# Attention backward for one query: the second half of a wide output product placed behind the V scores

One core of a Trainium2 chip. The metric is the time of one execution in device microseconds (us), lower is better. PE is the tensor engine, ACT the scalar engine, DVE the vector engine, SP the engine that issues the transfers; PSUM is the memory in which PE leaves its sums.

## The reference, cut to what matters

```python
# B = 1, H = 32 heads, Sq = 1 query, Skv = 8192 keys, Dh = 128, all bfloat16
def _fwd_reference(q, k, v):
    scale = q.shape[-1] ** -0.5
    scores = jnp.einsum('bhqd,bhkd->bhqk', q, k) * scale
    attn = _softmax(scores, axis=-1)
    return jnp.einsum('bhqk,bhkd->bhqd', attn, v)

def reference(q, k, v, grad_out):
    _out, _vjp = jax.vjp(_f, q, k, v)     # _f calls _fwd_reference
    return (_out, *_vjp(grad_out))        # out, dq, dk, dv
```

Per head, K and V (2.097 MB each) are read, and dK and dV, just as large, are written. With one query, dK and dV are outer products, and every other product has a vector on one side.

## The kernel before

The heads are a software pipeline: in pass `h`, the K work of head `h` is mixed with the dQ and dK work of head `h-1`, and then the V work of head `h` follows. The order of instructions on each engine is the order of the program text. All tile transfers are issued by one engine (SP), in program order; SP waits at each until its buffer or its data is ready.

The output of a head is the product of the probabilities with V. Most heads do it in 64 narrow matmuls with V as weights (`contract`). Nine "wide" heads (2, 5, 8, ... 26) take V as the moving operand in 16 matmuls of 4x512. The sum then stands in PSUM tile `s`, ACT copies it to `four`, and 8 KB go to scratch memory:

```python
    def o_wide(h, first, last):
        x = st[h]
        for g in range(first, last):
            nc.tensor.matmul(x["s"][0:R, :], lhsT=x["p"][:, R * g:R * (g + 1), 0],
                             rhs=Vt[h][:, R * g:R * (g + 1), :].rearrange("p n d -> p (n d)"),
                             start=(g == 0), stop=(g == NT // R - 1), skip_group_check=True)
        if last == NT // R:
            four = small.tile([R, R * D], F32, tag="four", name="four")
            nc.scalar.copy(four[:], x["s"][0:R, :])
            nc.sync.dma_start(scratch[WIDE.index(h), 0:R * R * D].rearrange("(a c) -> a c", a=R), four[:])
```

`s` has one buffer, V two, K three, and the gradient tiles dK and dV two each. The part of pass `h` that matters:

```python
        # ... K scores, softmax, first V transposes of head h; dQ, dK of head h-1 ...
        v_copy(h, 0)
        v_transposes(h, 1)                 # each is 8 transposes on PE and a copy on ACT
        if h in WIDE:
            o_wide(h, 0, 8)
        v_transposes(h, 2)
        if h in WIDE:
            o_wide(h, 8, 16)               # <- what moves
        else:
            contract(Vt[h], x["p"], x["m"][:, 2:3])
            nc.scalar.copy(o_all[:, h:h + 1], x["m"][:, 2:3])
        v_scores(h, 0)
        v_scores(h, 1)
        v_transposes(h, 3)
        # ... (a small matmul in plain heads)
        v_scores(h, 2)
        v_scores(h, 3)                     # waits for ACT's copy of the transposes 3
        outer(h, "dv", 0); outer(h, "dv", 1); outer(h, "dv", 2)      # DVE
        if 0 < h and h + 2 < H:
            load_v(h + 2)                  # needs V's buffer of head h
        outer(h, "dv", 3)                  # and the store of dV
        # next pass: rows_bc(h+1) writes `s` on PE, XK transposes on DVE,
        # pd_of(h) (a reduction of the V scores on DVE, then a matmul), K scores of h+1
```

## Time and profile before

| | |
|---|---|
| time, median of the first 3 runs | 646.6 us (646.49 to 646.83) |
| bytes moved, mean rate | 269.85 MB, 419 GB/s |
| busy share: main DMA queue, DVE, PE, ACT | 98.2%, 79%, 77%, 29% |

To read the pages: a strip has 40 slices of the span, 16.1 us each. In a chain or timeline a row is start, length, engine, line of the kernel, and output<-inputs; what ended an idle time before the row stands in brackets. L218 is the wide product, L206 the V scores, L194 the V transposes, L256 the row broadcast of the next head, L163 its K scores, L223 ACT's copy of the sum. A "DMA" row in the chain is the time from a transfer's issue to its landing.

### The profile page before, as it was taken

The page shows a single profiled execution, that of the slowest core. Times are in us where ns is not written, and L with a number is a line of the kernel's source. Part 1 is how long each engine was busy: PE and PEld are TensorE (multiplying, and loading weights), DVE is VectorE, ACT ScalarE, POOL GpSimd, SP SyncE. Part 2 cuts the span into 40 slices and gives each one's busy share as a digit, 9 for nine tenths or more (in the row PEclk, how much of TensorE's full clock was granted, in tenths as well). Part 3 has the DMA queues.
Part 4 walks back from the last instruction along what each step waited for, and adds up shares of the span by engine and source line. Part 5 has one row for each costly group of instructions (what it writes and reads, how often), then busy time and mean ns, then how long its engine had stood idle before and what let it go on. Part 6 is the DMA issues. An engine that isn't in the chain of part 4 may idle for free.

```text
span 644.6 us, 20121 instructions
## 1 busy us (share of the span) xinstructions
PE 495.5 (77%) x9242; PEld 432.6 (67%) x9242; DVE 508.7 (79%) x673; ACT 184.3 (29%) x333; POOL 0.7 (0%) x6
## 2 busy tenths in 40 slices
PE   3998888886777977788777788877787787877780
PEld 2886876785676776658665776767586666866670
DVE  5998989877977778877789777797777987778870
ACT  2333333322233231233222332313322133321230
POOL 0000000000000000000000000000000000000000
PEclk9768668765766765686558666666865586665665
DMA  8999999999999999999999999999999999999995
GB/s 349 406 426 432 425 423 428 427 429 427 430 427 429 426 432 424 430 428 425 430 425 430 429 428 427 430 425 429 428 430 426 429 427 430 428 429 428 426 379 213
DMA packets 19833, 269.85 MB, mean 419 GB/s; under 512 B 2397, under 2 KB 2433, under 8 KB 2981
## 3 DMA queue, kind: packets, MB, share of 16 engines
q1 hardware_dynamic: 19701, 268.56, 98.2%
q8 instruction: 72, 1.18, 0.7%
q14 instruction: 12, 0.10, 0.0%
q10 hardware_dynamic: 48, 0.01, 0.0%
HBM read 134.25 MB, written 134.31 MB: 417 GB/s over the span
## 4 chain that ended last, share of the span: by engine, by line
DMA 61%; PE 27%; DVE 7%; ACT 1%; issue 1%; SPq 0%; DVEq 0%; ACTq 0%
DMA Vt<-in_v_dram 60%; PE T_ps L194 15%; DVE XK_sb L152 3%; DVE G_dv L241 3%; PE s_ps L218 3%; PE m_ps L211 2%; PE dp_ps L206 2%; PE s_ps L163 2%; PE dp_ps L211 1%; DMA Kt<-in_k_dram 1%; PE m_ps L328 1%; DVE G_dk L241 1%; ACT XT_sb L185 0%; ACT p_rep L337 0%; PE s_ps L179 0%
## 5 line engine op out<-in xcount | busy, mean ns | idle before, releaser
L194 PE MATMUL T_ps<-ident_f,Vt 128*128 128x128 f32 x1024 | 209.5, 373 | 26.1 <-DMA Vt<-in_v_dram 24.4
L194 PEld LDWEIGHTS T_ps<-ident_f,Vt 128*128 128x128 f32 x1024 | 176.1, 201 | 44.8 <-PE m_ps L316 26.7
L241 DVE TENSOR_TENSOR G_dv<-p_rep,qd 128x2048 bf16<-128x2048 bf16 x128 | 148.2, 1220 | 58.8 <-DMA out_dram<-G_dv 48.2
L241 DVE TENSOR_TENSOR G_dk<-ds_rep,qd 128x2048 bf16<-128x2048 bf16 x128 | 155.7, 1219 | 1.6 <-DMA out_dram<-G_dk 0.5
L185 ACT COPY XT_sb<-T_ps 128x1024 f32<-128x1024 f32 x128 | 128.3, 1007 | 91.6 <-PE T_ps L194 88.0
L152 DVE STREAM_TRANSPOSE XK_sb<-Kt 128x1024 f32<-128x1024 f32 x128 | 149.3, 1217 | 6.2 <-DMA Kt<-in_k_dram 5.7
L163 PE MATMUL s_ps<-q_blk,XK_sb 128*128 128x4 bf16 x2048 | 59.6, 168 | 75.3 <-DVE pdt L265 68.2
L163 PEld LDWEIGHTS <-XK_sb 128*128 128x128 bf16 x2048 | 56.9, 104 | 82.7 <-DVE pdt L265 75.4
L206 PE MATMUL dp_ps<-do_blk,XT_sb 128*128 128x2 bf16 x2048 | 66.5, 164 | 19.7 <-ACT XT_sb L185 19.7
L206 PEld LDWEIGHTS <-XT_sb 128*128 128x128 bf16 x2048 | 63.7, 101 | 26.4 <-ACT XT_sb L185 22.4
L211 PE MATMUL dp_ps<-ds_rep,Kt 128*128 128x1 bf16 x2048 | 64.0, 165 | 0.0
L211 PEld LDWEIGHTS <-Kt 128*128 128x128 bf16 x2048 | 59.5, 104 | 5.4 <-issue 5.3
L275 ACT COPY dq_all<-dp_ps 128x1 f32<-128x1 f32 x32 | 5.1, 159 | 193.2 <-PE dp_ps L211 186.3
L211 PEld LDWEIGHTS <-Vt 128*128 128x128 bf16 x1472 | 41.3, 97 | 0.6
L211 PE MATMUL m_ps<-p_rep,Vt 128*128 128x1 bf16 x1472 | 40.8, 164 | 0.0
L218 PE MATMUL s_ps<-Vt,p_rep 128*4 128x512 bf16 x144 | 36.4, 398 | 0.0
L337 ACT ACTIVATE p_rep<-e,rinv 128x256 bf16<-128x256 f32 x32 | 16.3, 509 | 63.3 <-DVE rinv L335 63.3
L335 DVE RECIPROCAL rinv<-m_ps 128x1 f32<-128x1 f32 x32 | 5.4, 168 | 33.8 <-PE m_ps L328 33.7
L218 PEld LDWEIGHTS <-p_rep 128*4 128x4 bf16 x144 | 11.2, 87 | 20.1 <-issue 6.0
L260 ACT CAST qd<-s_ps 128x256 bf16<-128x256 f32 x32 | 11.9, 372 | 31.0 <-PE s_ps L256 31.0
L327 ACT ACTIVATE e<-s_ps,nbias 128x64 f32<-128x64 f32 x32 | 10.0, 314 | 32.2 <-DVE nbias L323 32.2
L169 DVE TENSOR_TENSOR sm<-s_ps,in_quad 128x256 f32<-128x256 f32 x32 | 13.6, 425 | 6.5 <-PE s_ps L163 3.6
(56 smaller groups left out, 191.4 us busy)
## 6 DMA issues: line engine op xcount, KB each, us to landing
Vt<-in_v_dram SPq DMA_DIRECT2D x32, 2048.0 KB
Kt<-in_k_dram SPq DMA_DIRECT2D x31, 2048.0 KB
out_dram<-G_dv SPq DMA_DIRECT2D x30, 2048.0 KB
out_dram<-G_dk SPq DMA_DIRECT2D x30, 2048.0 KB
out_dram<-G_dv SPq DMA_DIRECT2D x4, 1024.0 KB
out_dram<-G_dk SPq DMA_DIRECT2D x4, 1024.0 KB
Kt<-in_k_dram SPq DMA_DIRECT2D x4, 512.0 KB
scratch<-four SPq DMA_DIRECT2D x9, 8.0 KB
```

What stands on the lines that cost most here:

```text
L152: nc.vector.transpose(XK[h][:, :, :, u, :], slots(Kt[h], u, NCH).rearrange("p g d -> p (g d)").bitcast(F32).rearrange("p (g w j) -> p g w ...
L163: nc.tensor.matmul(out[:, g, :], lhsT=cols[:, g, c // 2, c % 2], rhs=q_blk[:, h, c, :], start=(c == 0), stop=(c == 2 * NB - 1), skip_group ...
L169: nc.vector.tensor_tensor(x["sm"][:], x["s"][:, 0:NT].rearrange("p (a g) -> p a g", a=NQ).unsqueeze(2) .to_broadcast([P, NQ, NCH, CH]), in ...
L185: nc.scalar.copy(X[:], st[h].pop("T")[:])
L194: nc.tensor.transpose(T_ps[:, i, :], words[:, m * P:(m + 1) * P], ident_f[:])
L206: nc.tensor.matmul(st[h]["dp"][:, n:n + 2], lhsT=X[:, i, e2, :], rhs=do_blk[:, h, e2, :], start=(e2 == 0), stop=(e2 == 1), skip_group_chec ...
L211: nc.tensor.matmul(out_col, lhsT=Xt[:, n, :], rhs=rep[:, n, 0:1], start=(n == 0), stop=(n == NT - 1), skip_group_check=True)
L218: nc.tensor.matmul(x["s"][0:R, :], lhsT=x["p"][:, R * g:R * (g + 1), 0], rhs=Vt[h][:, R * g:R * (g + 1), :].rearrange("p n d -> p (n d)"), ...
L241: nc.vector.tensor_tensor(slots(G, r, 4).rearrange("p n (a b) -> p n a b", b=R), slots(rep, r, 4).unsqueeze(2).to_broadcast([P, Q, D // R, ...
L260: nc.scalar.copy(x["qd"][:].rearrange("p a d -> p (a d)"), x["s"][:, 256:512])
L327: nc.scalar.activation(e[:], x["sn"], ACT.Exp, bias=nbias[:], scale=scale, accum_out=rs[:])
L337: nc.scalar.activation(x["p"][:], e[:].unsqueeze(2).to_broadcast([P, NT, R]), ACT.Copy, scale=rinv[:])
```

## The change

Its evident intent is to let the V scores start sooner, so that the reduction behind them doesn't wait. No work is added or removed.

```diff
@@ -342,9 +342,7 @@
         if h in WIDE:
             o_wide(h, 0, 8)
         v_transposes(h, 2)
-        if h in WIDE:
-            o_wide(h, 8, 16)
-        else:
+        if h not in WIDE:
             contract(Vt[h], x["p"], x["m"][:, 2:3])
             nc.scalar.copy(o_all[:, h:h + 1], x["m"][:, 2:3])
         v_scores(h, 0)
@@ -355,6 +353,8 @@
         v_scores(h, 2)
         v_scores(h, 3)
+        if h in WIDE:
+            o_wide(h, 8, 16)
         outer(h, "dv", 0)
```

## The prediction

> **What bounds the kernel now.** I first read the page's strips and its queue table, because they tell whether anything is saturated. The first strip is the busy share of the 16 DMA engines in 40 slices of 16.1 us.
>
> ```profile
> DMA  8999999999999999999999999999999999999995
> GB/s 349 406 426 432 425 423 428 427 429 427 430 427 429 426 432 424 430 428 425 430 425 430 429 428 427 430 425 429 428 430 426 429 427 430 428 429 428 426 379 213
> ...
> q1 hardware_dynamic: 19701, 268.56, 98.2%
> ```
>
> The transfers are at 90% or more from the second slice to the last but one, at an even 423 to 432 GB/s, and the one queue that carries all tiles takes 98.2% of the engines' time. No compute engine is near that (DVE 79%, PE 77%, ACT 29%). Per head the kernel moves four tiles of 2.097 MB (K and V in, dK and dV out), 8.389 MB; at 428 GB/s, the mean of each 100 us stretch from 100 to 600 us, that is 19.6 us a head, and 32 heads are 627 us. The remaining 19 us of the span are the slower first and last slices.
>
> Then I read the chain that ended last, in order of time, around one wide head (head 14, of 2, 5, 8, ... 26) and the plain heads on both sides of it. Columns: start us, length us, what.
>
> ```profile
> 303.97 30.30 DMA Vt<-in_v_dram
> ...
> 341.08 1.82 PE s_ps L218 x8
> 342.89 0.89 PE dp_ps L206 x32
> 343.78 0.95 PE T_ps L194 x8
> 344.73 0.02 issue
> 344.75 29.17 DMA Vt<-in_v_dram
> 373.92 0.14 issue
> ...
> 383.21 30.53 DMA Vt<-in_v_dram
> 413.74 0.14 issue
> ```
>
> The page puts 60% of the span on "DMA Vt<-in_v_dram", and these lines show why that must not be read as a latency: a 2 MB load takes 4.9 us of all engines (2.097 MB / 428 GB/s) but 29 to 30.5 us from issue to landing. The other 24 to 25 us are four or five earlier 2 MB transfers ahead of it. The loads land at 334.27, 373.92 and 413.74, that is 39.65 and 39.82 us apart, which is two heads' worth of bytes (16.78 MB / 428 GB/s = 39.2 us) within 2%. The decisive comparison: from the start of a head's V transposes to the issue of the next V load takes 9.16 us in a plain head (374.05 to 383.21) and 10.34 us in the wide head (334.41 to 344.75). The wide head already issues 1.2 us later, its load waits about 1.2 us less (29.17 against 30.30 and 30.53), and the landing comes in step all the same. **The queue is elastic: a later issue shortens the time in it.**
>
> **What the Trainium skill says.** "DMA: Bandwidth & Descriptors", section "Where 436 GB/s comes from", gives 435.2 GB/s as the ceiling of the 16 ports; the steady 428 GB/s here is 98% of it, so I take the transfers as saturated. The same page, "Queues, rings and completion order", says that descriptors on one engine are consumed in ring order; the trace agrees as far as it can, the V load of 323.89 landing at 354.2 and the dV store issued right after it (324.32) releasing its buffer at 359.2, one tile's 5 us later. "Perfetto Trace Analysis", "DMA Instruction — HWDGE (DVE, Sync)", says that the data movement lies outside the profiled window of the issuing instruction; the issues last 0.33 us here against 29 us to landing, so I judge by landings.
>
> **The change part by part.** Nothing is added or removed. Nine times, eight 128x512 matmuls move from before the V scores to behind the last, and with them ACT's copy of the sum and the 8 KB store that follow. The built order of the sync and vector queues is the same as before; ACT changes by one place (the copy of the sum moves behind the fourth XT copy), PE by the move itself. The tensor line around the place, before (start, length, engine, line):
>
> ```profile
> 341.01 1.89 PE L218 MATMUL s_ps<-Vt,p_rep 128*4 128x512 bf16 x8
> 342.83 0.95 PE L206 MATMUL dp_ps<-do_blk,XT_sb 128*128 128x2 bf16 x32
> 343.64 1.07 PE L194 MATMUL T_ps<-ident_f,Vt 128*128 128x128 f32 x8
> 344.55 0.54 PE L206 MATMUL dp_ps<-do_blk,XT_sb 128*128 128x2 bf16 x16
> 345.87 0.55 PE L206 MATMUL dp_ps<-do_blk,XT_sb 128*128 128x2 bf16 x16 [0.78 <-ACT XT_sb L185]
> 346.36 0.28 PE L256 MATMUL s_ps<-rows,ident 32*128 32x256 bf16 x1
> 347.85 0.38 PE L232 MATMUL m_ps<-pd,ones_s 128*128 128x1 f32 x2 [1.22 <-DVE pd L230]
> 349.01 0.35 PE L163 MATMUL s_ps<-q_blk,XK_sb 128*128 128x4 bf16 x7 [0.78 <-DVE pdt L265]
> ```
>
> - The eight matmuls take 1.82 us start to start (341.01 to 342.83), 228 ns each. Without them in front, the V scores, the last transposes and ACT's fourth copy all come 1.82 us sooner. Its inputs allow that: the third XT copy ends at 342.12 and the third scores would want it at about 342.7. The fourth copy still takes 1.01 us, so the gap of 0.78 us in front of the last scores stays: the moved matmuls stand behind that gap and do not fill it. The last scores would end near 346.4 - 1.8 = 344.55, the eight matmuls near 346.45.
> - ACT's copy of the sum (576 ns, from the row of that tile) then runs from 346.5 to 347.05 in place of 342.93 to 343.51.
> - **A new wait on PE.** The next head's row broadcast (346.36) writes the buffer that this copy reads, of which there is one. It moves to about 347.1, so 0.75 us of PE idleness is new per wide head, 9 x 0.75 = 6.8 us in all. But the matmul behind it waits until 347.85 for DVE anyway, so the broadcast (0.28 to 0.39 us) still fits and the K scores at 349.01 stay. ACT's cast of the broadcast comes 0.75 us later and is first used by the next head's outer products, microseconds after.
> - **A later release of V.** The moved matmuls become the last readers of the V tile. On the sync queue the 8 KB store comes first, then the V load, then the dV store. These issued at 343.53, 344.75 and 345.17; I expect 347.1, 347.4 and 347.8. Two 2 MB transfers thus start waiting 2.65 us later, nine times. The next K load (353.07) is untouched.
> - What of it lies on the path that sets the end: before the V load of 344.75 about 24 us of transfers are queued, and 24 - 2.65 is still over 20. The thinnest queue at a wide head is at head 2. Up to its V load at 57.70, thirteen tiles (27.3 MB) have been issued. By the strip some 23.1 MB have been moved (16.1 us each at 349, 406 and 426 GB/s, and 9.4 us at 432), which leaves 4.2 MB or 9.8 us, still over three times the delay. So the engines never run dry, the order is the same, and the bytes are the same: 0 us. The last wide head is 26, five heads from the end; the tail (V landing at 612.7, then the last stores) has no moved work.
>
> Sum: 9 x 2.65 = 24 us of later issues, all taken from waiting in the queue, and 6.8 us of new PE idleness beside DMA. On the end: 0, with a few tenths either way.
>
> **The rivals.**
> 1. *The chain of waits is right and the V load's 29 us are a fixed latency.* Then each later release would carry through. Wide heads alternate between the two V buffers, so each buffer's loop would take 4 or 5 of the 9 delays, 4.5 x 2.65 = 12 us, 658.5 us (+1.8%). The 60% speaks for it; the comparison of wide and plain heads above speaks against it. I give it about 1%.
> 2. *PE or DVE becomes the bound through the new buffer wait.* If the row broadcast held up the K scores by the whole 0.75 us, a head would lengthen by that much: 6.8 us, 653.4 us. The 1.2 us that PE waits for DVE behind it speaks against it, and so does DVE, which sits idle 48.2 us in 22 waits for dV stores: compute has slack to make a delay up in the same head.
> 3. *A gain from earlier V scores.* They end 1.8 us sooner, so the vector engine's reduction of them never waits. That wait is 2.3 us in 2 places, all told, and in early heads the new broadcast wait would give back about as much; behind saturated transfers it is worth 0.
> 4. *The dV store's delay holds up the dV product two heads later,* which waits for its buffer (the 48.2 us above). The store keeps its place in the queue, so it should land at the same time: 0.
>
> **Range and chances.** The estimate is the time before, 646.6 us. The three runs lay within 0.34 us. I allow about 0.15% for a slightly different mix of reads and writes in the queue and for the early heads: 645.7 to 647.6 us. Faster by over 2% needs fewer bytes or a better rate, neither touched: 0.5%. Slower by over 2% needs more than rival 1 in full: 0.5%.
>
> **What would show it right or wrong.** In the profile after: DMA share and GB/s strip unchanged; in the chain the V loads issued by wide heads shortened from about 29.2 to about 26.5 us with the landings still 39.6 to 39.8 us apart; the row broadcast at PE with a new wait of some 0.75 us for ACT's copy, near 7 us in nine; the three sync issues 2.6 to 3.6 us later within the head; the K scores not later. The prediction is wrong if landings move apart to 42 us after wide heads, if the DMA strip shows a slice under 9 in the middle, or if the K scores of the next head move by the new wait and DMA's rate falls with them.

## More of the kernel before

The granted clock is the share of its full speed that PE was allowed.

## The result, and the profile after

After: 646.03 us median of 4 runs (645.96 to 646.93); before in the same rounds 646.72 us (646.49 to 647.59). The ratio is 0.999, 95% interval 0.9973 to 1.0007: the same. A ratio is the mean time of one kernel's runs over that of the other's of the same rounds, so not quite the ratio of the medians.

The page after, strips of DMA share and GB/s, and the queue's row:

```profile
DMA  8999999999999999999999999999999999999985
GB/s 338 419 423 430 426 427 426 425 424 421 427 408 428 428 428 431 423 431 429 426 426 432 426 428 429 428 427 430 424 430 428 430 424 431 425 431 427 430 376 235
...
q1 hardware_dynamic: 19701, 268.56, 98.3%
```

The transfers are as busy as before. One slice, of 177 to 193 us, has 408 GB/s; no issue is late there, and I don't know its cause. The profiled run happens to be the slowest of the four (646.93 us).

The chain after, around the same wide head as in the prediction (start, length, what):

```profile
305.64 29.49 DMA Vt<-in_v_dram
...
345.25 0.55 PE dp_ps L206 x16
345.80 1.83 PE s_ps L218 x8
347.64 0.02 issue
347.66 0.58 ACT four L223
348.24 0.04 issue
348.29 0.26 PE s_ps L256
348.55 0.06 PE m_ps L232
348.61 26.85 DMA Vt<-in_v_dram
375.47 0.14 issue
...
384.76 29.59 DMA Vt<-in_v_dram
```

The head's last link before the V load is now scores, wide product, copy of the sum, row broadcast. The load is issued 13.35 us after the start of the head's V transposes (335.26) instead of 10.34 us, and it waits 26.85 us instead of 29.17: 3.0 us later in, 2.3 us shorter. Over the nine wide heads the two traces give 3.2 us later and 3.4 us shorter on average. (This head is head 17. The prediction calls it 14, a miscount of mine; nothing in the working depends on it.)

The tensor engine's timeline after, around the moved matmuls:

```profile
343.02 1.07 PE L194 MATMUL T_ps<-ident_f,Vt 128*128 128x128 f32 x8
343.93 0.54 PE L206 MATMUL dp_ps<-do_blk,XT_sb 128*128 128x2 bf16 x16
345.25 0.55 PE L206 MATMUL dp_ps<-do_blk,XT_sb 128*128 128x2 bf16 x16 [0.78 <-ACT XT_sb L185]
345.74 1.89 PE L218 MATMUL s_ps<-Vt,p_rep 128*4 128x512 bf16 x8
348.29 0.26 PE L256 MATMUL s_ps<-rows,ident 32*128 32x256 bf16 x1 [0.66 <-ACT four L223]
348.55 0.38 PE L232 MATMUL m_ps<-pd,ones_s 128*128 128x1 f32 x2
349.71 1.84 PE L163 MATMUL s_ps<-q_blk,XK_sb 128*128 128x4 bf16 x64 [0.78 <-DVE pdt L265]
```

The gap of 0.78 us in front of the last V scores is still there, and a new gap of 0.66 us stands in front of the row broadcast, which waits for ACT's copy of `s`. The broadcast is 1.1 us later within the head than before, but the matmul behind it had waited 1.22 us for DVE. The K scores come 14.45 us after the head's V start (335.26 to 349.71), before 14.60 us.

### The profile page after: what moved, and what is told of

It reads as the page before. It is cut to its first block, busy times and chain, and to the rows that moved or that the text cites. A ratio compares the mean times of both kernels' runs of the same rounds, so it can differ in the third digit from the quotient of the medians.

```text
span 644.9 us, 20121 instructions
## 1 busy us (share of the span) xinstructions
PE 501.1 (78%) x9242; PEld 435.4 (68%) x9242; DVE 509.1 (79%) x673; ACT 184.6 (29%) x333; POOL 0.7 (0%) x6
## 4 chain that ended last, share of the span: by engine, by line
DMA 59%; PE 29%; DVE 5%; ACT 2%; issue 1%; SPq 0%; DVEq 0%; ACTq 0%
DMA Vt<-in_v_dram 58%; PE T_ps L194 16%; PE s_ps L218 3%; PE m_ps L211 3%; PE dp_ps L206 3%; DVE XK_sb L152 2%; DVE G_dv L241 2%; PE s_ps L163 2%; PE dp_ps L211 1%; ACT XT_sb L185 1%; DMA Kt<-in_k_dram 1%; PE m_ps L328 1%; DVE G_dk L241 1%; ACT four L223 0%; ACT p_rep L337 0%
## 5 line engine op out<-in xcount | busy, mean ns | idle before, releaser
L194 PE MATMUL T_ps<-ident_f,Vt 128*128 128x128 f32 x1024 | 211.7, 376 | 26.4 <-DMA Vt<-in_v_dram 24.3
L194 PEld LDWEIGHTS T_ps<-ident_f,Vt 128*128 128x128 f32 x1024 | 177.6, 202 | 45.2 <-PE m_ps L316 18.7
L206 PEld LDWEIGHTS <-XT_sb 128*128 128x128 bf16 x2048 | 65.1, 102 | 22.1 <-ACT XT_sb L185 21.9
L218 PE MATMUL s_ps<-Vt,p_rep 128*4 128x512 bf16 x144 | 41.4, 440 | 0.0
L267 DVE SCALAR_TENSOR_TENSOR ds_rep<-dp_ps,pdt,p_s 128x256 bf16<-128x256 f32 x32 | 15.5, 484 | 3.5 <-PE dp_ps L206 0.5
```

The source lines that it names most:

```text
L194: nc.tensor.transpose(T_ps[:, i, :], words[:, m * P:(m + 1) * P], ident_f[:])
L206: nc.tensor.matmul(st[h]["dp"][:, n:n + 2], lhsT=X[:, i, e2, :], rhs=do_blk[:, h, e2, :], start=(e2 == 0), stop=(e2 == 1), skip_group_chec ...
L267: nc.vector.scalar_tensor_tensor(out=x["ds"][:], in0=x["dp"][:, 0:NT].unsqueeze(2).to_broadcast([P, NT, R]), scalar=pdt[:], in1=x["p_s"][: ...
```

## The experiments

The theory: the 16 DMA engines' bytes set the time. The moved matmuls make V and dV go out later, the queue in front of the transfers is shortened by that, and what the order does to compute is hidden. The expectations call this the queue theory. Its rivals: the wait behind a V load is a latency; or the order does change compute, but in two directions that cancel; or V's buffers are the bound.

### Both orders where the transfers don't bind

`light_before` and `light_after` store only the first quarter of each dK and dV tile. Most of those outputs is never written, so their results are wrong (out and dq remain right). All the compute is there.

```diff
-            nc.sync.dma_start(rows_of(dst, h, c, parts), slots(G, c, parts))
+            if r == 3:
+                nc.sync.dma_start(rows_of(dst, h, 0, 4), slots(G, 0, 4))
```

> The order of before with only a quarter of every dK and dV tile stored (wrong result on purpose), so 5.2 MB a head in place of 8.4 and about 12.3 us of transfers. Queue theory: the transfers stop binding and the heads run at the compute pace of the early heads before (16.4 us plain, 17.8 us wide), so about 555 us (545 to 570), and a V load lands within 5 to 12 us of its issue instead of 29. Fixed-latency rival: the V loads still take about 29 us from issue to landing and the time stays near 640 us.

> The same with the order of after. This shows what the move is worth where compute binds. By the early heads of the two traces, from the third V transposes of a wide head to the next K scores it is 7.93 us before and 7.72 after at equal clock: 9 x 0.2 = 1.9 us quicker than light_before (0.3%). Rival (the new wait for ACT's copy costs more than the earlier V scores give): 0.3 to 0.6 us slower per wide head, 3 to 5 us (0.5 to 1%). If the moved matmuls run at the lower clock more often than before, that adds up to 1.6 us per head to the slower side.

Measured: light_before 569.15 us (5 runs, 567.67 to 573.51), ratio to before 0.8816 (0.8790 to 0.8842); light_after 570.32 us (568.04 to 572.60), ratio 0.8818 (0.8796 to 0.8839). The page of light_before, its strip of GB/s and its chain by engine:

```profile
GB/s 339 402 415 329 317 312 246 250 343 325 286 288 304 331 342 290 286 300 266 339 324 284 291 307 326 346 266 302 295 288 348 315 275 269 306 329 315 289 72 78
...
PE 51%; DVE 40%; ACT 4%; issue 3%; DMA 1%; SPq 0%; DVEq 0%; ACTq 0%
```

With 100 MB less to move, 12% of the time goes, though no instruction of compute was taken away; DMA leaves the chain (61% to 1%). So the bytes bind in the full kernel. The landing of single V loads, of which the expectation speaks, is in no view of `prof` here, since nothing waits for them any more. But the packed trace keeps sixteen completion stamps for each 2 MB transfer, and the last of them is the landing that the chain shows (373.92 us for the V load of 344.75 in before). By these stamps the V loads issued in light_before after the first 20 us land 8.7 to 10.8 us after their issue (only the first takes 14.8), where before takes 28.4 to 31.2 us from head 6 on. The wait shrinks with the bytes, so it is no fixed latency. I had the time 14 us too low: the wide heads take 18.6 us on average, not 17.8, and some plain ones 18 to 19.

The two orders are equal here as well, and the trace shows two effects of opposite sign. From the first wide matmul of a head to the DVE copy that starts the next head's chain (`pdt`) it is 9.61 us in light_before whenever both groups run at full clock; the shortest in light_after is 9.56 us, with its first group a little slow (2.02 us), and in the full kernel after 9.43 us (head 5) against 9.61 before. That is the 0.2 us expected. But in light_after the moved group ran slow in three of nine heads. Its timeline in one of them:

```profile
418.19 0.55 PE L206 MATMUL dp_ps<-do_blk,XT_sb 128*128 128x2 bf16 x16 [0.78 <-ACT XT_sb L185]
418.67 3.34 PE L218 MATMUL s_ps<-Vt,p_rep 128*4 128x512 bf16 x8
422.68 0.26 PE L257 MATMUL s_ps<-rows,ident 32*128 32x256 bf16 x1 [0.66 <-ACT four L223]
```

Eight matmuls take 3.34 us here and 1.89 us elsewhere. In the full kernel after, such a group (3.45 us, from 227.02 us) lay in a stretch with a mean granted clock of 0.53, while another (345.74 us) had 1.00. In light_before the second group took 1.89 us in all nine heads. The mean over the nine heads, slow groups on either side included, is 9.93 us in light_before and 10.31 us in light_after. Nine times 0.38 us is 3.4 us, yet the profiled spans are 567.0 and 566.7 us: the rest of the heads took as much less, which this study doesn't explain. Whether the place behind the gap lowers the clock, or the phase of the throttle happened to fall so, one profile each doesn't settle.

### Between the third and the fourth scores

`light_between` and `full_between` put the second eight matmuls into the gap of 0.78 us.

```diff
         v_scores(h, 2)
-        v_scores(h, 3)
         if h in WIDE:
             o_wide(h, 8, 16)
+        v_scores(h, 3)
```

> The same with the second eight matmuls between the third and the fourth V scores, in the gap of 0.78 us that the fourth scores wait for ACT's copy. Expected 0.5 us per wide head quicker than light_after, 4 to 5 us (0.8%), as the gap is filled and the copy of the sum no longer stands in front of the row broadcast. Rival: DVE's own chain binds there and it is equal to light_before within 1 us.

> That order with all stores. Queue theory: the same as before and after, 646.5 us within 0.8, whatever light_between shows, since the transfers still bind. Rival (compute order carries to the end): as much quicker as light_between is, 4 to 5 us.

Measured: light_between 556.95 us (4 runs, 556.19 to 559.22), ratio 0.8620 (0.8604 to 0.8636), so 12 us under light_before. full_between 645.84 us (645.82 to 645.96), correct, ratio to before 0.9989 (0.9976 to 1.0003): the same. The tensor engine in a wide head of light_between:

```profile
206.76 0.54 PE L206 MATMUL dp_ps<-do_blk,XT_sb 128*128 128x2 bf16 x16
207.23 1.89 PE L218 MATMUL s_ps<-Vt,p_rep 128*4 128x512 bf16 x8
209.05 0.55 PE L206 MATMUL dp_ps<-do_blk,XT_sb 128*128 128x2 bf16 x16
209.78 0.26 PE L257 MATMUL s_ps<-rows,ident 32*128 32x256 bf16 x1 [0.18 <-ACT four L223]
```

Both gaps are gone or nearly so: the scores wait no more for ACT (their copy runs beside the wide product), and the broadcast waits 0.18 us for the copy of the sum. From the first wide matmul to `pdt` it is 8.66 us at full clock, 0.95 under light_before, 9.04 us on average. That is 9 x 0.9 = 8 us of the 12. From K scores to K scores, 10 us of the 12 are in the wide heads (18.55 and 17.43 us on average) and 2 us in the plain ones, for which I have no cause. I had expected 4 to 5 us. **This is the sharpest pair: an order that is worth 12 us where compute binds is worth nothing that can be told from the spread (0.8 us, interval over 1) where the bytes bind.**

### A third V buffer

```diff
-V_BUFS = 2
+V_BUFS = 3
```

> Before with three V buffers in place of two, so V is released far ahead and its load can be issued a head earlier. Queue theory: the load only waits longer, time 646.6 within 1.5 us. Fixed-latency rival (V's release to landing is the loop that binds): a large gain, 20 to 30% of the span.

Measured: 646.56 us (646.40 to 646.68), before in the same rounds 646.56 us, ratio 0.9999 (0.9984 to 1.0014). V's buffers are not the bound, although 60% of the chain goes through V loads. The load did only wait longer: the last V load was issued 7.6 us earlier than in before (574.90 and 582.51 us) and landed at the same time (612.93 and 612.73 us).

### All V loads later

`late_v` is the order of before, with the V loads moved behind the next pass's K load.

```diff
@@ behind the K load of pass h
+        if 1 < h and h + 1 < 26:
+            load_v(h + 1)
@@ where the V load was
-        if 0 < h and h + 2 < H:
+        if 0 < h and h + 2 < H and h + 2 >= 26:
             load_v(h + 2)
```

> The order of before, but every V load up to head 25 is issued behind the next head's K load, some 8 to 9 us later, in plain and wide heads alike. Queue theory: the wait from issue to landing shrinks by as much as the issue is late (to about 20 us), landings stay about 39.7 us apart, time 646.6 us within 2. Fixed-latency rival: each of the two V loops takes 11 or 12 delays of 8.5 us: about 740 us.

Measured: 651.32 us (651.22 to 651.70), ratio 1.0075 (1.0058 to 1.0092). V loads on its chain:

```profile
162.03 23.26 DMA Vt<-in_v_dram
202.09 23.61 DMA Vt<-in_v_dram
243.61 21.72 DMA Vt<-in_v_dram
```

They wait about 7 us less, and the time is 89 us below what a fixed latency would make of it: that rival falls. But it isn't free, as I had expected within 2 us: 4.8 us were lost. What is known of this loss follows below.

### How much later is too late

`fill50` and `fill130` take the order of after and put 50 or 130 more 128x256 matmuls on V in front of the moved eight, in wide heads only, into columns of `m` that nobody reads. The results are correct.

```diff
+            for g in range(50):     # or 130
+                nc.tensor.matmul(x["m"][0:R, 256:512], lhsT=x["p"][:, R * (g % 16):R * (g % 16 + 1), 0],
+                                 rhs=Vt[h][:, 2 * (g % 32):2 * (g % 32 + 1), :].rearrange("p n d -> p (n d)"),
+                                 start=True, stop=True, skip_group_check=True)
             o_wide(h, 8, 16)
```

> The order of after with 50 further 128x256 matmuls from V in front of the moved eight, in the nine wide heads only (their sums are never read; the result stays right). At 114 ns each (half of the 228 ns of a 128x512) that is 5.7 us more PE time on the path to the V release and to the next head. Three heads take 3 x 19.8 = 59.4 us by the transfers and 2 x 16.4 + 17.8 = 50.6 us by compute, so 8.8 us of slack per wide head: the same within 1%. Rival (the release is on the path): 9 x 5.7 / 2 = 26 us slower, or 51 us if a delay stops the whole head.

> The same with 130: 14.8 us per wide head, 6 us more than the slack. Queue theory: compute now binds from the time at which the lead is used up, 9 x 6 = 54 us, less a lead of 10 to 20 us: 675 to 700 us, and the strip of the transfers shows gaps. If the time stays at 647 us the slack is larger than worked out.

Measured: fill50 656.99 us (656.52 to 657.98), ratio 1.0163 (1.0147 to 1.0178); fill130 708.72 us (706.49 to 712.49), ratio 1.0967 (1.0928 to 1.1005). The first missed its expectation, the same within 1%. The second confirms that compute then binds: DMA has 4% of its chain, PE 56% and DVE 31%. It is slower than expected. Even without the lead of 10 to 20 us that I had taken off, the sum gives 700.6 us; the other 8 us were not followed up. In its strip every wide head makes a hole (fill130, DMA share and GB/s):

```profile
DMA  8998799799979997999899799969996999799997
GB/s 356 411 427 361 278 420 423 316 356 424 423 315 404 419 428 299 418 423 404 319 420 422 316 404 418 427 254 413 423 421 232 421 422 422 282 417 426 421 426 317
```

Why did fill50 lose 10 us, with compute still under 59.4 us for three heads? First I made a balance of the queue from the traces: bytes issued (the issue times with their sizes) less bytes moved (the rates of windows of 1 us, less 1.3 MB of other transfers, spread evenly). In bytes waiting just before a V load is issued:

| | before | after | fill50 |
|---|---:|---:|---:|
| head 2 | 4.3 MB | 2.7 MB | 0.6 MB |
| head 17 | 8.0 MB | 6.9 MB | 2.6 MB |
| head 26 | 7.0 MB | 5.7 MB | 1.7 MB |

fill50 keeps SP waiting from 523.29 to 540.85 us in head 26. Nothing is issued in 17.5 us, which is 7.5 MB of transfers at 428 GB/s; in the wide head of after the like stretch is 11.8 us (336.46 to 348.26), before 8.1 us. The rates in windows of 2 us of fill50, from the V load's issue at 541.21 on (the last columns are granted clock, DMA share, GB/s):

```profile
541.00:543.00 2.00, 1.85 (x59) 1.71 (x59) 1.44 (x3) 0.37 (x1) 0.00 (x0) 1.00 0.90 306
543.00:545.00 2.00, 2.00 (x75) 1.81 (x73) 1.98 (x4) 0.00 (x0) 0.00 (x0) 0.79 0.92 386
545.00:547.00 2.00, 1.96 (x25) 1.91 (x23) 1.97 (x6) 0.46 (x3) 0.00 (x0) 0.50 1.10 434
547.00:549.00 2.00, 2.00 (x11) 2.00 (x11) 1.53 (x4) 0.96 (x4) 0.00 (x0) 0.50 0.90 336
```

With 1.7 MB left the rate falls. The queue doesn't have to be empty for that, since the 16 engines don't run out together. The completion stamps show it, if each is one engine's: of the dK store issued at 523.29 us six came by 541.9 us, just as the V load went out, and the last at 558.5 us. The first six stamps of that V load follow 7.3 to 7.7 us after these six, instead of some 4.9 us with a full queue. It is no sharp limit: fill50 lost bytes against before at heads 2, 23 and 26 (0.6 to 1.9 MB left), but not at head 5 (1.8 MB). That gave a new theory for fill50's loss, late issues, against the plain delay of compute. Two runs test it.

### Late issues, or late compute?

`fill50_free` puts the 50 matmuls behind the moved eight, and they read a constant in place of V, so that V and dV go out on time.

```diff
             o_wide(h, 8, 16)
+            for g in range(50):
+                nc.tensor.matmul(x["m"][0:R, 256:512], lhsT=x["p"][:, R * (g % 16):R * (g % 16 + 1), 0],
+                                 rhs=do_blk[:].rearrange("p h e t -> p (h e t)")[:, 0:128].unsqueeze(1)
+                                 .to_broadcast([P, 2, 128]),
+                                 start=True, stop=True, skip_group_check=True)
```

> The order of after with the 50 further 128x256 matmuls behind the moved eight and reading a constant, so V and the dV store go out at the time of after and only the next head's compute comes 5.6 us later. If fill50 lost its 10 us because the late issues let the queue run short (0.5 to 3.6 MB were left at its nine late V issues), this run loses little: 647 to 650 us, with 3 MB or more left at every V issue behind head 2. Rival: the loss came from the compute delay itself, and this run is as slow as fill50, 657 us.

`fill50_v3` is fill50 with three V buffers and the V load issued early in the head.

```diff
-V_BUFS = 2
+V_BUFS = 3
@@
         v_transposes(h, 1)
+        if 0 < h and h + 2 < H:
+            load_v(h + 2)
@@
         outer(h, "dv", 2)
-        if 0 < h and h + 2 < H:
-            load_v(h + 2)
```

> fill50 as it was, with the same matmuls on V in the same place, but three V buffers and each V load issued some 12 us earlier in the head, so that up to 2 MB more are queued when the long stretch without issues comes. Queue theory: most of the 10 us comes back, 647 to 650 us, although the wide heads compute as long as in fill50 (24 to 25 us). Rival (compute delay): 657 us.

Measured: fill50_free 653.47 us (653.22 to 654.05), ratio 1.0108 (1.0091 to 1.0125); fill50_v3 656.02 us (655.44 to 656.61), ratio 1.0145 (1.0130 to 1.0160). Both correct, both misses: a third of the loss comes back in the first, next to nothing in the second. The theory of late issues alone falls. What the traces show in its place, against before:

| | K scores of head 31 start later by | span longer by | bytes short at 600 us | lead at the last V load, before 3.2 MB |
|---|---:|---:|---:|---:|
| late_v | 4.7 us | 4.7 us | 1.54 MB = 3.6 us | 3.8 MB (+1.4 us) |
| fill50_free | 6.7 us | 6.7 us | 0.55 MB = 1.3 us | 4.6 MB (+3.3 us) |
| fill50 | 9.9 us | 10.0 us | 2.37 MB = 5.5 us | 4.9 MB (+4.0 us) |
| fill50_v3 | 9.7 us | 9.6 us | 1.06 MB = 2.5 us | 5.2 MB (+4.7 us) |

First, the span ends 36.6 to 37.1 us after the last head's K scores start, in every run with all stores but fill130 (35.9 us). The tail is the last head's own softmax, products and stores, with the DMA at 379 and 213 GB/s before. So what counts is how late the last head is reached. Second, that lateness has two parts. One is the bytes not moved by then, through stretches with a thin queue. The other I call the lead: when a V load lands, its bytes and all that were issued ahead of it have moved, and some bytes of tiles issued later have moved as well. Those go from 1.3 MB at 135 us to 3.2 MB at 613 us before, and grow faster in the runs with more matmuls. A tile lands when its last engine is through, so I read the lead as fast engines running ahead of a slow one. The two parts give 5.0, 4.6, 9.5 and 7.2 us against the 4.7, 6.7, 9.9 and 9.7 us measured; some 2 us of fill50_free and fill50_v3 stay unexplained.

The completion stamps bear this reading out and show more. In before the first and the last stamp of a V load are 1.0 us apart at 14 us and 14.6 us apart at 613 us. For the last V load of each run (us):

| | first stamp | 15th | 16th, the landing | landing later than before by |
|---|---:|---:|---:|---:|
| before | 598.1 | 611.6 | 612.7 | |
| late_v | 604.3 | 614.0 | 617.4 | 4.7 |
| fill50_free | 599.3 | 614.6 | 619.5 | 6.8 |
| fill50 | 607.3 | 613.8 | 622.7 | 10.0 |
| fill50_v3 | 601.4 | 613.2 | 622.4 | 9.7 |

The landing is as late as the span is longer. But the fifteenth stamp is only 1.7 to 3.1 us later than in before; the rest of the lateness is the last one alone. It did not lack work in fill50_free and fill50_v3: from 30 to 585 us the next tile was issued at least 9.3 us before the last stamp of the tile ahead of it. So the first table is an account of bytes and not a cause, and what made these two runs slow was neither a thin queue nor a wait for compute: the last of the sixteen fell behind with work waiting. The trace does not say which engine a stamp belongs to, and why the last is slower there is not shown.

For the change itself these parts are small: at 600 us after is 0.43 MB short of before (1.0 us, most of it in the slice with 408 GB/s), its lead at the last V load is 3.1 MB, and head 31 is reached 0.74 us later in the profiled runs (0.23 us of which it had from the first head on). The timed runs show the two kernels equal, after 0.1% ahead if anything.

No version beats both kernels. full_between is the best where compute binds, but with all stores its interval reaches over 1.

## Why the prediction was right

- **The bound.** The bytes of the 16 engines, at the pace of the last of them, set the time: shown by light_before (100 MB less, 12% of the time less, same compute) and by light_between against full_between. v3_before shows that it is not V's buffers. (A slip in the working: 644.6 us of span less 627 leave 17.6 us for the ends, not 19.)
- **The elastic queue.** Read off wide and plain heads before, and shown by after (3.0 us later, 2.3 us less wait at head 17; 3.2 and 3.4 on average), by light_before (landings in 8.7 to 10.8 us) and by late_v (waits of 21 to 24 us in place of 29 to 31).
- **Sizes of the move.** The issues within the head came 3.9, 3.0 and 3.0 us later (predicted 3.6, 2.65, 2.65), for head 17's first wide group took 0.3 us longer. The new wait on PE was 6.0 us in nine (predicted 6.8), beside DVE work, and the K scores did not come later. DVE's wait for the V scores (2.3 us in 2 places) is gone, as rival 3 said, and DVE now waits 2.9 us in 3 places for the matmul behind the broadcast, which it also said.
- **What was mis-sized: the depth of the queue.** The step "four or five earlier 2 MB transfers ahead of it", 24 us, took all of the 29 us less the load's own 4.9 us as queue. The balance shows 8.0 MB, 18.7 us, and a lead of 2.3 MB, 5.4 us; with the load's own time that makes 29.0 of the 29.17 us. The reserve at most heads was thus a quarter smaller than stated. It did not matter, since 6 MB and more were left at most wide heads, and at head 2, where I had counted in bytes, 4.2 MB stated were 4.3 MB found and 2.7 MB left after.
- **What was off in the signs named: the landings.** They were to stay 39.6 to 39.8 us apart. Around head 17 they are 40.3 and 38.9 us apart in after, while four heads take 79.2 us (335.13 to 414.35) as against 79.5 before. The rate is the same; why they are uneven, the runs don't tell.
- **What was not foreseen:** that the moved group would at times run at about half clock (3.25 to 3.45 us for 1.89). Behind the transfers it shows as the K scores of head 12 starting 1.9 us later than before after such a group; by head 15 that was down to 0.7 us. Nor was it foreseen that one of the sixteen completions falls ever further behind, which is what a longer delay met: fill50_free, with 5.6 us per wide head, lost 6.9 us. That is no proof against rival 2's "compute has slack to make a delay up", since tiles were waiting in its queue throughout.

## What to carry to other kernels

When a chain of waits runs through a DMA, compare the time to landing with what the bytes take: if it is several times longer, and late issues land in step with early ones, the bytes are the bound, and moving compute about is worth nothing until bytes are saved. Before moving the last reader of a buffer to a later place, count in bytes what is still queued at the end of the longest stretch without an issue: here 2.7 MB were enough, and with under 2 MB the rate fell at three heads of four. Look also at how far the last completion of a transfer lags behind the others, since the transfer lands with it. To find out what an order is worth at all, thin out the transfers on purpose and time it there: it was 12 us in the light kernel, hidden in the full one.

## What the Trainium skill lacked or had wrong

- "DMA: Bandwidth & Descriptors" ("Queues, rings and completion order") has no figure for how far the engines drift apart in a long saturated run. In the kernel before, the first and the last completion stamp of a 2 MB load are 1.0 us apart at 14 us and 14.6 us apart at 613 us, and up to 22.3 us in fill50_v3. At the landing, 1.3 to 3.2 MB of later tiles had moved in before, and up to 6.0 MB in the slowed kernels, by a balance of issued and moved bytes.
- The same page says nothing of how much must be queued to keep the rate. Here it held with 2.7 MB waiting (head 2 of after), and fell to 306 GB/s with 1.7 MB (head 26 of fill50).
- "Perfetto Trace Analysis" ("Identifying Dependency Chains") doesn't warn that a chain counts queueing as a wait for the load: 60% of the span stood at V loads here, and a third V buffer changed the time by 0.0%.
